# Attention and FFN on one core: the first batch's FFN units given out later, and three batches' units pinned in program order

## The chip, the cores and the metric

The kernel runs on one core of one Trainium2 chip. The metric is device time in microseconds (us) of one execution; several runs are taken and their median is quoted. The engines are named as in the profile: PE is TensorE's matmul, PEld its weight load, DVE is VectorE, ACT is ScalarE, POOL is GpSimd, and SP is SyncE, whose queue issues the DMAs.

## What is computed

Eight batches of eight heads, 576 positions, head width 64: attention weights are kept only within `tau` of the row's maximum. The result, as 4608 tokens of width 512, goes through a feed-forward network (FFN) of two layers with width 2048 between them.

```python
scores = scale * np.matmul(q, k.transpose(0, 1, 3, 2))
thresh = np.max(scores, axis=-1, keepdims=True) - tau
scores = np.where(scores >= thresh, scores, -1000000000.0)
scores = scores - np.max(scores, axis=-1, keepdims=True)
attn = np.exp(scores)
attn = attn / (np.sum(attn, axis=-1, keepdims=True) + 1e-09)
attn_out = np.matmul(attn, v)
x = np.ascontiguousarray(attn_out.transpose(0, 2, 1, 3)).reshape(B * S, H * D)
h = x @ w_in
g = h * (1.0 / (1.0 + np.exp(-h)))
out = g @ w_out
```

## The kernel before

**Attention** works in tiles of 128 query rows by 576 keys. A tile `t` goes through `scores` (PE: line 456 in batch 0, line 468 later), `soft1` (DVE, line 478: the maximum), `soft1b` (ACT, line 488: exp), `soft2` (DVE, line 497: mask, multiply and sum), `soft2b` (ACT line 515, or POOL line 511: divide by the sum) and `soft3`. In batch 0 `soft3` transposes on PE (lines 407 and 412) and copies out on ACT (lines 420 and 421); in later batches POOL splits the tile in two float16 halves (lines 523 to 529) and a DMA transposes them (line 539). `av` multiplies with V (line 430 in batch 0, line 554 later), and `av_post` (lines 572 and 573) writes a pair of heads into `x16`, the input of the FFN. `x16` has two buffers, so batch b+2 can write it only when the first layer of batch b is done. Score tiles have two PSUM buffers, exp tiles four.

**The FFN** of one range of token columns is cut in 32 units of 12 matmuls. An `h_unit` (first layer, line 597) makes one block of 128 hidden features; its `post` is tanh on ACT (line 607), a product on DVE (line 608), a float16 copy on ACT (line 614) and the rest on DVE (line 615). An `o_unit` (second layer, line 630) is a quarter of one block of 128 outputs; after the fourth quarter ACT scales it into `wst` (line 642) and SP stores it. Batches 0 and 1 come in ranges of 256 and 320 columns, the others in two of 288. From batch 1's second range on, a range's second layer is held back and handed out in turn with the next range's first layer (`held`).

**The order** is written in one loop over `t` (lines 792 to 842). There are 301 tile places: batch 0's tiles stand at 0 to 15 and 28 to 47, batch 1's at 49 to 84, then 36 a batch; 16 to 27 and 48 are empty. The loop body gives out `scores(t + 1)`, the steps of the tiles around `t`, the loads and splits that are due, and as many FFN units as `credit` allows. `credit` grows by `rate` at each place. When a range becomes ready (batch 0's at places 20 and 52, batch 1's at 69 and 89, batch 2's at 125 and 126), `rate` is set to the units listed, over the places to the next range, times 0.95; batch 0's two ranges take `RATES` instead. The weights of the two layers are loaded, decoded and split in the same loop (`W_PLAN`: the second layer's are split at places 22 to 36, lines 224 and 225).

A scheduler then orders each engine's instructions by priority and by its own clock, so an engine's order is not that of the loop: scores have a high priority, FFN units none. For batches below `PACED` the first matmul of a unit is pinned behind what stands ahead of it on PE in program order:

```python
if b < PACED and k == 0:
    tc.keep_in_program_order(mm)
```

Units of other batches may be moved ahead of scores, or behind them.

Of the kernel before, what the change touches and what calls it, by code (L numbers as in the profile page):

```python
# [24 lines left out]
NF = DFF // P  # L25
# [5 lines left out]
LOAD = 5  # L31
AV_LAG = 3
GAP, GAP1 = 12, 1
PACED = 1
RATES = (1.03, 1.45)
RATE = 0.95

W_PLAN = ((0, 0, 10, 13, 0), (16, 9, 22, 36, 0))
# [14 lines left out]
def attention_moe(  # L53
# [46 lines left out]
    for i in range(2):  # L100
        t = const.tile([P, S + 64], F32R, name=f"qstack{i}")
# [268 lines left out]
    for kind, base, n in (("low", 4096, 256), ("high", 5120, 320)):  # L370
        for i in range(2):
            t = gbuf.bitcast(F32)[:, base + 2 * n * i : base + 2 * n * (i + 1)]
# [71 lines left out]
    def scores(t):  # L444
        v, parts = tiles[t]
        s_ps = ps_s.tile([P, 2, 512], F32, tag="s", name=f"s_{t}")
        sps[t] = s_ps
        if v in direct:
            (h, i, _, _) = parts[0]
            qt, kt = direct[v]  # L450
            if visits[v][2] == "low":
                o = (h % 2) * 256 + i * P
            else:
                o = (h % 2) * 384 + (i - 2) * P
            for j in range(2):
                nc.tensor.matmul(  # L456
                    s_ps[:, j, :HALF], qt[:, o : o + P],
                    kt[:, j * HALF : (j + 1) * HALF], start=True, stop=True,
                )
            return  # L460
        seq = [
            (qstack[h % 2][:, qcol(h, i) : qcol(h, i) + P], kk)
            for h, i, _, _ in parts
            for kk in khl[h]
        ]
        for n, (lhs, kk) in enumerate(seq):
            for j in range(2):
                nc.tensor.matmul(  # L468
                    s_ps[:, j, :HALF], lhs, kk[:, j * HALF : (j + 1) * HALF],
                    start=(n == 0), stop=(n == len(seq) - 1),  # L470
                )

    def soft1(t):
        s_ps = sps[t]
        sm = sb.tile([P, 5], F32, tag="small", name=f"sm_{t}", bufs=4)
        w = sb.tile([P, S], F32, tag="w32", name=f"w32_{t}", bufs=4)
        negm = sm[:, 0:1]
        nc.vector.tensor_reduce(  # L478
            out=negm, in_=s_ps[:, :, :HALF], op=ALU.max, axis=AX.XY, negate=True
        )  # L480
        nc.vector.tensor_scalar(
            out=sm[:, 1:2], in0=negm, scalar1=-1.0, scalar2=ntau, op0=ALU.mult, op1=ALU.add
        )
        small[t] = sm
        wtile[t] = w

    def soft1b(t):
        nc.scalar.activation(  # L488
            wtile[t].rearrange("p (j c) -> p j c", j=2), sps[t][:, :, :HALF], AF.Exp,
            bias=small[t][:, 0:1],  # L490
        )

    def soft2(t):
        s_ps = sps.pop(t)
        sm, w = small[t], wtile[t]
        w3 = w.rearrange("p (j c) -> p j c", j=2)
        nc.vector.scalar_tensor_tensor(  # L497
            out=w3, in0=s_ps[:, :, :HALF], scalar=sm[:, 1:2], in1=w3,
            op0=ALU.is_ge, op1=ALU.mult, accum_out=sm[:, 2:3],
        )  # L500
        nc.vector.tensor_scalar(
            out=sm[:, 3:4], in0=sm[:, 2:3], scalar1=1e-9, scalar2=2.0**-12,
            op0=ALU.add, op1=ALU.mult,
        )
        nc.vector.reciprocal(out=sm[:, 4:5], in_=sm[:, 3:4])  # L505

    def soft2b(t):
        w = wtile[t]
        r = small.pop(t)[:, 4:5]
        if tiles[t][0] in direct and not 12 <= t < first_high + 10:  # L510
            nc.gpsimd.tensor_scalar(
                out=w, in0=w, scalar1=r, scalar2=1.0, op0=ALU.mult, op1=ALU.mult
            )
        else:
            nc.scalar.activation(w, w, AF.Copy, scale=r)  # L515
# [74 lines left out]
    def h_unit(b, c0, n, f, own=None):  # L590
# [4 lines left out]
        for c in range(NK):  # L595
            for lo_w, lo_x in ((0, 0), (0, 1), (1, 0)):
# [3 lines left out]
                )  # L600
                if b < PACED and k == 0:
                    tc.keep_in_program_order(mm)
# [20 lines left out]
    def o_unit(b, c0, n, d, quarter, own=None):  # L623
        if quarter == 0:
            po[b, c0, d] = bank([P, 512], f"o_{b}_{c0}_{d}", own)
        ps = po[b, c0, d]
        for f in range(4 * quarter, 4 * quarter + 4):
            g = gt[b, c0, f]
            for k, (lo_w, lo_g) in enumerate(((0, 0), (0, 1), (1, 0))):
                mm = nc.tensor.matmul(  # L630
                    ps[:, :n], wo(f, d, lo_w), g[:, lo_g, :n],
                    start=(f == 0 and k == 0), stop=(f == NF - 1 and k == 2),
                )
                if b < PACED and f == 4 * quarter and k == 0:
                    tc.keep_in_program_order(mm)

        def post():
            if quarter < 3:
                return

            o = wst[:, NW + d % 2, :]
            nc.scalar.activation(o[:, :n], ps[:, :n], AF.Copy, scale=moe_sc[b][:, 1:2])  # L642
            c = b * S + c0
            nc.sync.dma_start(out=outT[d * P : (d + 1) * P, c : c + n], in_=o[:, :n])

        return post
# [6 lines left out]
    def o_units(b, c0, n, owns=(None,)):  # L653
        return [
            lambda d=d, quarter=quarter: o_unit(b, c0, n, d, quarter, owns[d % len(owns)])
            for d in range(DM // P) for quarter in range(4)
        ]

    held = []

    def moe_units(b, c0, n):
        if b == 0 and c0 == 0:
            return h_units(b, c0, n, (0, 2)) + o_units(b, c0, n, (0, 2))
        if b == 0 or (b == 1 and c0 == 0 and 1 in HALVED):
            return h_units(b, c0, n) + o_units(b, c0, n)
        out = []
        if held:
            for pair in zip(h_units(b, c0, n, (0, 1)), o_units(*held.pop(), (2,))):
                out.extend(pair)
        else:  # L670
            out = h_units(b, c0, n)
        held.append((b, c0, n))
        return out
# [12 lines left out]
    start = {}  # L686
# [37 lines left out]
    NT = len(tiles)  # L724
# [17 lines left out]
    def pri(offset, f):  # L742
        def g():
            if offset == 0:
                return f()
            with tc.high_priority(offset=offset):
                return f()

        return g
# [22 lines left out]
    units = []  # L772
    post = []
    credit = 0.0
    rate = 0.0

    def run_posts():
        for f in post:
            f()
        post.clear()  # L780

    def step_unit():
        p = units.pop(0)()
        run_posts()
        post.append(p)

    def live(t):
        return 0 <= t < NT and tiles[t] is not None

    scores(0)  # L790
    t = 0
    while t < NT + 8 or units or ready or held:
        while ready and ready[0][0] <= t:
            _, b, c0, n = ready.pop(0)
            units.extend(moe_units(b, c0, n))
            nxt = [r[0] for r in ready if r[0] > t + 1]
            rate = len(units) / max(1, (nxt[0] if nxt else NT + 8) - t)
            rate *= RATE
            if b == 0:
                rate = RATES[0 if c0 == 0 else 1]  # L800
        if held and not ready and not units and t >= NT + 8:
            units.extend(o_units(*held.pop()))
        if t >= first_high + 20:
            turn[1] = 3
        if live(t):
            pri(PRI_SOFT1, lambda: soft1(t))()
        if live(t + 1):
            pri(PRI_S, lambda: scores(t + 1))()
        if live(t - 1):
            soft2b(t - 1)  # L810
        if live(t):
            pri(PRI_SOFT1, lambda: soft1b(t))()
        if live(t - 1) and tiles[t - 1][0] not in direct:
            soft3(t - 1)
        if live(t - 2) and tiles[t - 2][0] in direct:
            soft3(t - 2)
        for f in todo.pop(t, []):
            f()
        credit += rate
        if t >= NT:  # L820
            credit = max(credit, 4.0)
        if units and credit >= 1:
            step_unit()
            credit -= 1
        if live(t):
            pri(PRI_SOFT2, lambda: soft2(t))()
        for v, p, c0, n in avs.pop(t, []):
            b = visits[v][0]
            if v in direct:
                a_ps = av_direct(v, p)  # L830
            else:
                a_ps = pri(PRI_AV, lambda v=v, p=p, c0=c0, n=n: av(v, p, c0, n))()
            run_posts()
            scale = xscale if v in direct else 2.0**-12
            post.append(lambda b=b, p=p, c0=c0, n=n, a_ps=a_ps, scale=scale: av_post(b, p, c0, n, a_ps, scale))
        while units and credit >= 1:
            step_unit()
            credit -= 1
        if not units:
            credit = 0.0  # L840
            run_posts()
        t += 1
# [44 lines left out]
```

## Time and profile before

| | |
|---|---|
| median of 3 runs | 1228.99 us (1227.8 to 1229.81) |
| the profiled execution | 1226.58 us |
| its span, first to last instruction | 1224.8 us |
| PE busy | 1155.2 us, 94% of the span |
| DVE busy | 920.7 us, 75% |
| ACT busy | 808.4 us, 66% |
| POOL busy | 694.6 us, 57% |
| TensorE's granted clock, mean | 0.99 of full speed |

The profiled execution takes 1.8 us more than its span. Busy times are unions: two overlapping instructions of an engine count once. A stage's row gives its length, then each engine's busy time and, in brackets, how many instructions it ran. The k-th instruction of line 497 on DVE belongs to the k-th tile that is not empty, so its start tells when the kernel is at that tile; the stages of the rows below are cut at such starts, of tiles 28, 32, 44, 49, 52, 64, 84, 104, 125, 176 and 300.

### The profile page before, as it was taken

What the parts mean: (1) busy time and instruction counts of PE and PEld (TensorE: products, weight loads), DVE (VectorE), ACT (ScalarE), POOL (GpSimd) and SP (SyncE); (2) the same over time, 40 slices, a digit from 0 to 9 for tenths busy, and PEclk for the clock granted to TensorE, in tenths of its full rate; (3) what the DMA queues carried; (4) which work ended last, traced back from release to release, by engine and by line L of the source; (5) the groups of instructions that cost most, each with busy time, mean ns of one, the idle gap of its engine ahead of it and who ended that gap; (6) DMA issues with size and microseconds to landing.
All of it is one profiled execution on the core that took longest, in us unless ns stands there. A gap on an engine that the chain in (4) does not pass through costs nothing.

```text
span 1224.8 us, 27015 instructions
## 1 busy us (share of the span) xinstructions
PE 1155.2 (94%) x9474; PEld 902.3 (74%) x9474; DVE 920.7 (75%) x2625; ACT 808.4 (66%) x1519; POOL 694.6 (57%) x888
## 2 busy tenths in 40 slices
PE   6778998999999899999999999999999999999998
PEld 4546685777876677777877777787788877777777
DVE  7987949968989788899888888896788867333330
ACT  6679846967868676777777677785777756333331
POOL 2264226987877786877878658781787567000000
PEclk9999999999999999999999999999999999999999
DMA  9740127787896787787777748772888357100000
GB/s 313 264 133 28 51 58 180 155 167 159 152 172 128 168 148 136 146 154 172 142 145 145 162 96 171 142 136 82 137 159 141 84 103 122 26 11 16 15 11 25
DMA packets 340887, 151.73 MB, mean 124 GB/s; under 512 B 305936, under 2 KB 317200, under 8 KB 340752
## 3 DMA queue, kind: packets, MB, share of 16 engines
q1 hardware_dynamic: 340752, 150.01, 57.9%
q8 instruction: 75, 1.23, 0.4%
q14 instruction: 60, 0.49, 0.1%
HBM read 66.19 MB, written 9.44 MB: 62 GB/s over the span
## 4 chain that ended last, share of the span: by engine, by line
PE 54%; DVE 16%; DMA 9%; POOL 8%; ACT 6%; issue 6%; SPq 0%; POOLq 0%; ACTq 0%; DVEq 0%
PE o L630 20%; PE h L597 18%; PE s L468 7%; PE a L554 6%; DMA wT<-hl 5%; DVE w L497 4%; DVE sm L478 3%; DVE qstack L354 3%; POOL hl L526 2%; POOL hl L523 2%; ACT w L515 2%; ACT w L488 1%; PE s L456 1%; DMA vraw<-in_vL 1%; POOL wst L229 1%
## 5 line engine op out<-in xcount | busy, mean ns | idle before, releaser
L597 PE MATMUL h<-x,wst 128*128 128x288 f16 (+2 forms) x3072 | 423.4, 287 | 8.9 <-DVE gbuf L615 6.8
L630 PE MATMUL o<-gbuf,wst 128*128 128x288 f16 (+2 forms) x3072 | 418.5, 286 | 2.2 <-ACT wst L642 0.7
L597 PEld LDWEIGHTS <-wst 128*128 128x128 f16 x3072 | 292.1, 98 | 99.1 <-issue 21.0
L630 PEld LDWEIGHTS <-wst 128*128 128x128 f16 x3072 | 293.2, 98 | 82.3 <-issue 5.3
L526 POOL TENSOR_TENSOR hl<-w,hl 128x512 f16<-128x512 f32 x252 | 303.8, 1206 | 11.9
L523 POOL TENSOR_SCALAR hl<-w 128x576 f16<-128x576 f32 x252 | 171.7, 684 | 178.3 <-ACT w L515 140.6
L497 DVE SCALAR_TENSOR_TENSOR w<-s,sm,w 128x576 f32<-128x576 f32 x288 | 231.8, 812 | 47.1 <-ACT w L488 44.2
L488 ACT ACTIVATE w<-s,sm 128x576 f32<-128x576 f32 x288 | 210.9, 740 | 77.1 <-DVE sm L478 34.0
L478 DVE TENSOR_REDUCE sm<-s 128x1 f32<-128x576 f32 x288 | 215.2, 751 | 47.1 <-PE s L468 38.2
L515 ACT ACTIVATE w<-w,sm 128x576 f32<-128x576 f32 x266 | 201.6, 771 | 46.2 <-DVE sm L505 45.3
L607 ACT ACTIVATE th<-h,msc 128x288 f32<-128x288 f32 (+2 forms) x256 | 127.5, 499 | 110.4 <-PE h L597 109.2
L608 DVE SCALAR_TENSOR_TENSOR h<-th,h 128x288 f32<-128x288 f32 (+2 forms) x256 | 116.2, 456 | 109.9 <-ACT th L607 108.2
L468 PE MATMUL s<-khi,qstack 128*128 128x288 f32 x560 | 143.4, 336 | 9.3 <-DVE w L497 8.6
L614 ACT ACTIVATE gbuf<-h 128x288 f16<-128x288 f32 (+2 forms) x256 | 104.1, 408 | 71.9 <-DVE h L608 70.5
L615 DVE SCALAR_TENSOR_TENSOR gbuf<-h,gbuf 128x288 f16<-128x288 f32 (+2 forms) x256 | 115.3, 451 | 41.6 <-ACT gbuf L614 41.1
L554 PE MATMUL a<-wT,v 128*64 128x288 f16 (+2 forms) x1568 | 118.6, 292 | 12.9 <-DMA wT<-hl 12.7
L468 PE MATMUL s<-klo,qstack 128*128 128x288 f32 x560 | 120.7, 296 | 0.0
L364 POOL TENSOR_TENSOR klo<-kraw,khi 128x576 fp32r<-128x576 f32 x64 | 93.0, 1453 | 45.1 <-ACT khi L362 32.5
L554 PEld LDWEIGHTS <-v 128*64 128x64 f16 x1568 | 86.7, 111 | 36.8 <-issue 26.6
L468 PEld LDWEIGHTS s<-khi,qstack 128*128 128x128 f32 x560 | 87.3, 189 | 29.3 <-issue 15.3
L468 PEld LDWEIGHTS s<-klo,qstack 128*128 128x128 f32 x560 | 90.0, 188 | 0.8 <-issue 0.2
L529 POOL TENSOR_TENSOR hl<-w,hl 128x64 f16<-128x64 f32 x252 | 90.3, 358 | 0.0
(101 smaller groups left out, 905.5 us busy)
## 6 DMA issues: line engine op xcount, KB each, us to landing
kraw<-in_kT SPq DMA_DIRECT2D x128, 144.0 KB, 2.9
qraw<-in_qT SPq DMA_DIRECT2D x96, 144.0 KB, 3.0
vraw<-in_vL SPq DMA_DIRECT2D x32, 320.0 KB, 3.8
out_t<-wst SPq DMA_DIRECT2D x48, 144.0 KB, 2.1
gbuf<-in_w_in SPq DMA_DIRECT2D x12, 512.0 KB, 7.2
wT<-hl SPq DMA_TRANSPOSE x280, 3.3
wraw<-in_w_out SPq DMA_DIRECT2D x8, 512.0 KB, 4.5
gbuf<-in_w_out SPq DMA_DIRECT2D x8, 512.0 KB, 4.9
```

The lines of the kernel that those rows point to most:

```text
L468: nc.tensor.matmul(s_ps[:, j, :HALF], lhs, kk[:, j * HALF : (j + 1) * HALF], start=(n == 0), stop=(n == len(seq) - 1),)
L478: nc.vector.tensor_reduce(out=negm, in_=s_ps[:, :, :HALF], op=ALU.max, axis=AX.XY, negate=True)
L488: nc.scalar.activation(wtile[t].rearrange("p (j c) -> p j c", j=2), sps[t][:, :, :HALF], AF.Exp, bias=small[t][:, 0:1],)
L497: nc.vector.scalar_tensor_tensor(out=w3, in0=s_ps[:, :, :HALF], scalar=sm[:, 1:2], in1=w3, op0=ALU.is_ge, op1=ALU.mult, accum_out=sm[:, 2:3],)
L515: nc.scalar.activation(w, w, AF.Copy, scale=r)
L523: nc.gpsimd.tensor_scalar(out=fl[:, 0:S], in0=w, scalar1=1.0, scalar2=1.0, op0=ALU.mult, op1=ALU.mult)
L526: nc.gpsimd.tensor_tensor(out=fl[:, 640:1152], in0=w[:, 0:512], in1=fl[:, 0:512], op=ALU.subtract)
L554: nc.tensor.matmul(a_ps[odd * D : (odd + 1) * D, :n], vt[:, lo_v, odd, kv, :], wT[v, b * H + 2 * p + odd][:, kw, c0 - base : c0 - base + n ...
L597: mm = nc.tensor.matmul(ph[:, :n], wi(c, f, lo_w), x16[b, lo_x][:, c, c0 : c0 + n], start=(k == 0), stop=(k == 11),)
L607: nc.scalar.activation(th[:, :n], ph[:, :n], AF.Tanh, scale=moe_sc[b][:, 0:1])
L608: nc.vector.scalar_tensor_tensor(out=ph[:, :n], in0=th[:, :n], scalar=1.0, in1=ph[:, :n], op0=ALU.add, op1=ALU.mult,)
L630: mm = nc.tensor.matmul(ps[:, :n], wo(f, d, lo_w), g[:, lo_g, :n], start=(f == 0 and k == 0), stop=(f == NF - 1 and k == 2),)
```

## The change

Batch 0's first range is given out at 0.25 units a place in place of 1.03, its second at 1.75 in place of 1.45. The units of batches 1 and 2 take a rate of at most 1.75, which counts 16 held units too, and are pinned as batch 0's were. A held second layer is put on the list as soon as the list is empty, up to place 121 (batch 3's first tile). No instruction's work changes, and none is added or removed. The line numbers of the changed kernel are larger by one from line 35 on.

```diff
-PACED = 1
-RATES = (1.03, 1.45)
+PACED = 3
+TOP = 1.75
+RATES = (0.25, 1.75)
 RATE = 0.95
...
             nxt = [r[0] for r in ready if r[0] > t + 1]
-            rate = len(units) / max(1, (nxt[0] if nxt else NT + 8) - t)
+            more = NF if 0 < b < PACED else 0
+            rate = (len(units) + more) / max(1, (nxt[0] if nxt else NT + 8) - t)
             rate *= RATE
             if b == 0:
                 rate = RATES[0 if c0 == 0 else 1]
+            elif b < PACED:
+                rate = min(rate, TOP)
+        if held and not units and t < start[PACED, 0]:
+            units.extend(o_units(*held.pop(), (2,)))
```

The order of the engines shows what moves. In the rows, `w32_37` is tile 37's exp tile, `h_0_0_5` the sixth first-layer unit of batch 0's first range, `o_0_0_1` the second output block of that range; the last number is a buffer's.

**ACT around tile 37.** Before:

```order
L488 ACTIVATE w32_37_1508<-s_37_1459,sm_37_1507 128x576
L224 ACTIVATE wst_89<-wst_89,o_w_sc_989 128x512
L515 ACTIVATE w32_36_1456<-w32_36_1456,sm_36_1455 128x576
L614 ACTIVATE gbuf_61<-h_0_0_5_1060 128x256
L224 ACTIVATE wst_89<-wst_89,o_w_sc_989 128x512
L420 ACTIVATE wT_5_2_1429<-tm_35_1516 128x4x64
L421 ACTIVATE wT_5_2_1429<-tl_34_1469 128x128
L488 ACTIVATE w32_38_1547<-s_38_1511,sm_38_1546 128x576
L607 ACTIVATE th_0_0_6_1118<-h_0_0_6_1082,msc_0_770 128x256
L224 ACTIVATE wst_89<-wst_89,o_w_sc_989 128x512
L515 ACTIVATE w32_37_1508<-w32_37_1508,sm_37_1507 128x576
L607 ACTIVATE th_0_0_7_1150<-h_0_0_7_1105,msc_0_770 128x256
```

And in the changed kernel, from the same tile:

```order
L489 ACTIVATE w32_37_1279<-s_37_1243,sm_37_1278 128x576
L422 ACTIVATE wT_5_2_1213<-tl_33_1211 128x128
L399 ACTIVATE gbuf_61<-gbuf_61,gate_79 64x320
L608 ACTIVATE th_0_0_3_1273<-h_0_0_3_1218,msc_0_770 128x256
L225 ACTIVATE wst_89<-wst_89,o_w_sc_958 128x512
L516 ACTIVATE w32_36_1240<-w32_36_1240,sm_36_1239 128x576
L421 ACTIVATE wT_5_2_1213<-tm_35_1287 128x4x64
L489 ACTIVATE w32_38_1304<-s_38_1282,sm_38_1303 128x576
L422 ACTIVATE wT_5_2_1213<-tl_34_1253 128x128
```

Unit 3 of batch 0 stands where units 5 to 7 stood. From tile 32's exp to tile 44's, ACT had 12 instructions of line 607 and 13 of line 614; it now has 3 and 5.

**ACT around tile 47**, where batch 0's tiles end. Before:

```order
L488 ACTIVATE w32_46_1855<-s_46_1822,sm_46_1854 128x576
L421 ACTIVATE wT_6_5_1720<-tl_42_1787 128x128
L420 ACTIVATE wT_7_6_1834<-tm_43_1827 128x4x128
L614 ACTIVATE gbuf_61<-h_0_0_15_1434 128x256
L642 ACTIVATE wst_89<-o_0_0_0_1475,msc_0_770 128x256
L642 ACTIVATE wst_89<-o_0_0_1_1638,msc_0_770 128x256
L421 ACTIVATE wT_7_6_1834<-tl_43_1832 128x128
L488 ACTIVATE w32_47_1909<-s_47_1858,sm_47_1908 128x576
```

In the changed kernel, from the same tile on:

```order
L489 ACTIVATE w32_46_1543<-s_46_1522,sm_46_1542 128x576
L421 ACTIVATE wT_7_6_1534<-tm_44_1551 128x4x128
L422 ACTIVATE wT_7_6_1534<-tl_43_1532 128x128
L489 ACTIVATE w32_47_1590<-s_47_1546,sm_47_1589 128x576
L421 ACTIVATE wT_7_6_1534<-tm_45_1595 128x4x64
L422 ACTIVATE wT_7_6_1534<-tl_44_1556 128x128
L489 ACTIVATE w32_49_1653<-s_49_1627,sm_49_1652 128x576
```

The exp of tile 47 stood behind two second-layer results, each of 48 matmuls; nothing of the FFN stands ahead of it now. On PE, 348 FFN matmuls stood ahead of tile 52's scores; now 84 do.

**ACT after tile 177's exp**, in the changed kernel:

```order
L608 ACTIVATE th_2_288_12_7351<-h_2_288_12_7304,msc_2_5587 128x288
L615 ACTIVATE gbuf_61<-h_2_288_12_7304 128x288
L608 ACTIVATE th_2_288_13_7475<-h_2_288_13_7423,msc_2_5587 128x288
L615 ACTIVATE gbuf_61<-h_2_288_13_7423 128x288
L608 ACTIVATE th_2_288_14_7528<-h_2_288_14_7483,msc_2_5587 128x288
L615 ACTIVATE gbuf_61<-h_2_288_14_7483 128x288
L608 ACTIVATE th_2_288_15_7581<-h_2_288_15_7536,msc_2_5587 128x288
L615 ACTIVATE gbuf_61<-h_2_288_15_7536 128x288
L643 ACTIVATE wst_89<-o_2_0_3_7376,msc_2_5587 128x288
```

These are four of the twelve first-layer units between the exps of tiles 176 and 178, the last four of batch 2 (two units stood there before); four units of batch 3 and batch 4's first `x16` follow them, then tile 178's exp. PE has 1920 FFN matmuls ahead of tile 176's scores (2259 before) and 2249 ahead of tile 180's (2312 before). From tile 216 on the two counts differ by at most 49; ahead of tile 300's scores stand 4687 of the 6144 (4642 before).

## Rows read from the trace of the kernel before

**Rows 1.** The page's head: span, and busy time, share and instructions of PE.

```profile
span 1224.8 us, 27015 instructions
PE 1155.2 (94%) x9474; PEld 902.3 (74%) x9474; DVE 920.7 (75%) x2625; ACT 808.4 (66%) x1519; POOL 694.6 (57%) x888
```

**Rows 2.** Busy time by stage: PE, PEld, DVE, ACT, POOL; granted clock, DMA share, GB/s.

```profile
0.00:78.60 78.60, 57.78 (x345) 38.22 (x346) 66.59 (x204) 51.71 (x98) 22.48 (x34) 0.93 0.83 275
78.60:99.70 21.10, 14.51 (x93) 9.76 (x91) 12.78 (x47) 16.11 (x32) 16.84 (x18) 1.00 0.08 23
99.70:150.40 50.70, 45.87 (x295) 32.67 (x296) 43.40 (x117) 44.88 (x102) 16.02 (x15) 0.97 0.14 40
150.40:171.30 20.90, 20.90 (x182) 18.42 (x180) 8.47 (x27) 8.22 (x22) 2.99 (x4) 1.00 0.10 30
171.30:185.60 14.30, 13.45 (x107) 10.15 (x106) 10.23 (x29) 10.39 (x23) 6.50 (x9) 1.00 0.34 84
185.60:229.90 44.30, 37.46 (x271) 25.62 (x269) 41.98 (x116) 33.46 (x63) 32.60 (x39) 0.96 0.80 177
229.90:296.20 66.30, 65.02 (x553) 51.07 (x552) 52.88 (x155) 47.94 (x87) 56.26 (x72) 1.00 0.82 164
296.20:359.30 63.10, 59.56 (x527) 50.21 (x524) 59.39 (x174) 48.87 (x90) 52.53 (x66) 1.00 0.87 166
359.30:430.00 70.70, 62.93 (x511) 47.47 (x512) 59.55 (x177) 50.45 (x90) 51.14 (x66) 0.98 0.73 144
430.00:594.90 164.90, 159.84 (x1346) 125.70 (x1344) 146.57 (x424) 123.50 (x224) 126.61 (x166) 0.99 0.77 151
594.90:1035.50 440.60, 431.94 (x3725) 345.03 (x3724) 366.50 (x1049) 313.46 (x570) 306.61 (x401) 1.00 0.68 131
1035.50:1224.80 189.30, 185.93 (x1543) 148.01 (x1540) 52.33 (x118) 59.42 (x130) 3.98 (x6) 1.00 0.07 20
```

**Rows 3.** The same stages, first layer alone (line 597), then second layer alone (line 630).

```profile
99.70:150.40 50.70, 18.28 (x151) 14.82 (x152) 0.97 0.14 40
150.40:171.30 20.90, 2.29 (x20) 1.66 (x17) 1.00 0.10 30
185.60:229.90 44.30, 21.03 (x138) 13.41 (x139) 0.96 0.80 177
...
150.40:171.30 20.90, 15.02 (x132) 12.84 (x132) 1.00 0.10 30
171.30:185.60 14.30, 6.08 (x55) 5.29 (x55) 1.00 0.34 84
```

**Rows 4.** Groups by line and shape, PE, 1060 to 1200 us, and that stretch.

```profile
L630 PE MATMUL o<-gbuf,wst 128*128 128x288 f16 x581 | 76.6, 286 | 0.0
L597 PE MATMUL h<-x,wst 128*128 128x288 f16 x564 | 74.5, 286 | 0.0
...
1060.00:1200.00 140.00, 140.00 (x1145) 111.82 (x1144) 43.56 (x95) 48.49 (x106) 0.00 (x0) 1.00 0.04 14
```

**Rows 5.** Groups by line and shape, whole span: one unit's post at 256 columns.

```profile
L607 ACT ACTIVATE th<-h,msc 128x256 f32<-128x256 f32 x32 | 15.3, 480 | 3.9 <-PE h L597 3.7
L608 DVE SCALAR_TENSOR_TENSOR h<-th,h 128x256 f32<-128x256 f32 x32 | 13.4, 420 | 5.6 <-ACT th L607 5.6
L614 ACT ACTIVATE gbuf<-h 128x256 f16<-128x256 f32 x32 | 12.5, 392 | 3.2 <-DVE h L608 3.1
L615 DVE SCALAR_TENSOR_TENSOR gbuf<-h,gbuf 128x256 f16<-128x256 f32 x32 | 13.3, 414 | 0.4 <-ACT gbuf L614 0.3
```

**Rows 6.** Waits between 150.4 and 171.3 us: us in total, times, longest.

```profile
ACT wst L642 <- PE o L630: 10.0, 2, 5.2
DVE w L497 <- ACT w L488: 9.7, 4, 9.1
```

**Rows 7.** PE's own waits between 185.6 and 1035 us.

```profile
PE a L554 <- DMA wT<-hl: 12.7, 12, 2.4
PE s L468 <- DVE w L497: 8.6, 10, 2.6
```

## The prediction, made before the changed kernel ran

> **What bounds the kernel now.** I read the page's head first [rows 1]: PE is busy 1155.2 of 1224.8 us, so 69.6 us of the span are PE's idle time. No instruction is added or taken away, so the change can only move that idle time, at first order. Where it lies is read from busy time by stage [rows 2]: length less PE's busy time gives 20.8 us before 78.6 us, 6.6 up to 99.7, 4.8 up to 150.4, none up to 171.3, 0.9 up to 185.6, 6.8 up to 229.9, 1.3, 3.5 and 7.8 in the three stages up to 430, 5.1 up to 594.9, 8.7 up to 1035.5, and 3.4 in the last. The last stage is the reason why all of it counts: from 1035.5 us, with the last tiles through, PE works off the FFN for 189.3 us, 185.9 of them busy, while DVE has 52.3 us of work. A us of FFN that PE does not do earlier stands at the end, unless it fills a gap. In that part PE runs at its best: 1145 matmuls of 288 columns in 140 us without a gap [rows 4], 122 ns each, so 109 ns at 256 columns and 136 at 320.
>
> Three readings from the stages that the change touches. From 99.7 to 150.4 us (tiles 32 to 44, with the split of the second layer's weights) three engines share the load: PE 45.9, ACT 44.9 and DVE 43.4 of 50.7 us [rows 2]. From 150.4 to 171.3 us PE is never idle while DVE and ACT work 8.5 and 8.2 of 20.9 us; 132 second-layer matmuls run here [rows 3], and the waits say what stands still: ACT waits 10.0 us for second-layer results, and DVE once 9.1 us for an exp [rows 6], which is behind them in ACT's queue, as the order shows. From 185.6 to 229.9 us DVE is busy 42.0 of 44.3 us: it is the bound there, with PE idle for 6.8.
>
> **The early stretch, tiles 28 to 52.** The order shows 264 FFN matmuls fewer ahead of tile 52's scores (348 to 84), all of 256 columns: 264 x 0.109 = 28.7 us of PE's work go out and are done later. The question is whether this stretch becomes as much shorter.
> - *78.6 to 99.7 us*: ahead of tile 32's scores only 9 matmuls leave, and POOL's weight split (16.8 of 21.1 us) stays. I take 0.
> - *99.7 to 150.4 us*: by ACT's order 9 tanh and 8 copies leave, 9 x 0.480 + 8 x 0.392 = 7.5 us [rows 5]; DVE loses some 9 posts, 9 x (0.420 + 0.414) = 7.5; PE 75 matmuls, 8.2. The three fall together, so I take 7.5 us off. Least, half of it counts because the transposes, copies and scores of a tile wait for each other in turn: 4. Most, the whole stage shrinks with PE's share, 45.9 to 37.7 us at 90%: 9.
> - *150.4 to 171.3 us*: without the second-layer block what is left is DVE's work less one post, 8.5 - 0.8 = 7.6 us, the longest of the four. At 90% that takes 8.5 us, so 12.4 come off. Bounds: 10.3 (at 72%, DVE's share in the stage behind, it takes 10.6) and 13.3 (no gap).
> - *171.3 to 185.6 us*: 43 of 55 second-layer matmuls go, but DVE and ACT keep 10.2 and 10.4 us and gain a post. At 85% to 90% that is 12.2: 2.1 us off, between 0 and 3.5.
>
> Sum: 22.0 us off (14.3 to 25.8) against 28.7 us of PE's work put off. The early stretch costs 28.7 - 22.0 = **6.7 us**, between 2.9 and 14.4. Queues: SP loses two early groups of stores, which stood ahead of batch 1's loads and transposes; four stores come back around tiles 65 to 73. I count this at nothing, within the bounds.
>
> **Tiles 52 to 64.** DVE's order has the same steps of batch 1's start, and now the first range's posts in place of the second's. PE has 157 FFN matmuls in place of 156, but of 256 columns instead of mostly 320: 120 x 0.027 = 3.2 us less. The posts are shorter too, by about 0.1 us each, ten of them: 1.3 us. DVE is the bound, so **1.9 us** more of PE stay idle; between -1 and 5, the last if first-layer units wait for PSUM behind V's splits on DVE (the order puts posts 7 and 8 around them).
>
> **Tiles 64 to 176.** The pace is alike: 1679 FFN matmuls now (241 to 1920), 1755 before (504 to 2259). PE is the bound at 98%, 94%, 89% and 97% of the four stages [rows 2]; the hole is 359.3 to 430 us, 7.8 us idle, where batch 1's second range was paced at 0.475 units a place and now gets 1.478. An even supply may fill some of it. What ended PE's waits there speaks against much: 12.7 us for transposed tiles and 8.6 for a score buffer over the whole run of the attention [rows 7], neither a lack of FFN work. I take **-2 us**, between -8 and +3.
>
> **The catch-up, tiles 177 to 180.** What was put off is worked off when batch 4 needs `x16`: some 300 matmuls with few scores between. ACT's order has twelve first-layer units between two exps there. Attention stands still for 300 x 0.122 = 37 us, as it did in the block at 150.4 to 171.3 us, where PE had no gap. It costs nothing beyond work already counted, 0 to 2 us if the attention restarts slowly. From tile 216 on the counts differ by at most 49.
>
> **Sum.** 6.7 + 1.9 - 2 = **+6.6 us**. The profiled execution takes 1226.6 us, 2.4 less than the median of 1229.0; the change is added to the median: 1235.6 us. All low ends together give -6.1, all high ends +24.4.
>
> **The rivals.**
> - *Even pacing pays (faster).* Place: tiles 84 to 176, idle 16.4 us in all [rows 2]. With batches 1 and 2 pinned behind the scores, PE meets FFN units and scores alternately, and the late transposes find a unit ahead of them. It decides from about 8.6 us of recovered idle time on. If 10 come back and the early stretch costs 3 and tiles 52 to 64 nothing: -7, 1222 us. For it: idle time is clustered where the old pace was thinnest. Against: the waits named above are for data.
> - *No change.* The early stretch shrinks nearly as PE's work does (2.9), and 2 to 4 us come back later: 1229 us.
> - *Pinned units stand behind late scores (slower still).* For some 100 tiles a unit can't pass scores that wait for their buffer. If each costs what the present waits do over 12 more occasions, 12 x 0.86 = 10 us: 1246 us. Against: scores have two buffers, and batch 0's units are pinned already.
> - *The clock.* Between 0 and 78.6 us PE is busy 57.8 of 78.6 us, 74%, and the granted clock is 0.93; at 90%, from 99.7 to 150.4 us, it is 0.97 [rows 2], so part of a thin stretch is at 1.2 instead of 2.4 GHz. PE's share from tile 32 to 52 goes from 93% (80.2 of 85.9 us) to 51.5 / 63.9 = 81%. A mean of 0.93 is 14% of the time at the lower level: 9 of 63.9 us, which lose some 4.5 us of PE's work if nothing hides them: 1240 us. The Trainium skill, "TensorE: Matmul & The Clock Gate", section "HAM oscillation — how this bites in real kernels", has a rule against such a change: gaps in PE's work make the array fall back to the half rate, and the next burst starts slow. By it the early stretch would cost 11 us in place of 6.7. In this trace the 74% stretch bears it out only weakly, at a clock of 0.93.
>
> That the change doesn't do what it says is ruled out by the order: the units move as described.
>
> **How the numbers follow.** A measurement here can tell about 0.2% (2.5 us) from no change. My forecast, slower by 6.6 us, has 0.41; pinned units behind scores 0.10, the clock 0.05; no change 0.17; even pacing 0.27. Slower together 0.56, same 0.17, faster 0.27. The range reaches down to 1218, past the even-pacing case, and up to 1250, past the pinned case; less than 1 in 10 is left on either side.
>
> **What would show it.** Right: tile 52's mask (line 498 on DVE) starts near 164 us instead of 185.6; no wait of 9 us for an exp before it; PE idle time up to there near 40 us (33.1 before); a stretch near tile 178 in which PE has no gap for some 37 us and DVE works about half; tile 300's some 12 us later, as 45 matmuls fewer are left for the end. Wrong: tile 52 at 158 us or earlier, or after 170; PE idle between tiles 84 and 176 under 8 us (faster), or over 25 (pinned units); a granted clock under 0.93 between tiles 32 and 64.

## The result, and the profile after

The changed kernel takes 1246.83 us (median of 4 runs, 1242.78 to 1249.26) where the kernel before takes 1228.67 (4 runs): 1.0144 times the time, 95% interval 1.0115 to 1.0172, so 18 us slower. The profiled execution took 1242.78 us with a span of 1241.0, 16.2 us above the span of before; the ledger below is made against that.

The page's head of the changed kernel, against [rows 1]:

```profile
span 1241.0 us, 27028 instructions
PE 1157.3 (93%) x9474; PEld 904.3 (73%) x9474; DVE 921.6 (74%) x2625; ACT 810.0 (65%) x1519; POOL 688.6 (55%) x888
```

The work is the same; PE's idle time is 83.7 us in place of 69.6, and 2.1 us went into busy time. Busy time by stage of the changed kernel, columns as in [rows 2], cut at the same tiles (176 to 180 is a stage of its own here):

```profile
78.70:99.50 20.80, 14.78 (x93) 9.79 (x91) 12.23 (x47) 16.07 (x32) 16.86 (x18) 1.00 0.08 23
99.50:146.20 46.70, 36.69 (x190) 24.28 (x191) 38.51 (x100) 39.59 (x86) 14.72 (x14) 0.89 0.13 37
146.20:154.50 8.30, 7.53 (x51) 5.19 (x50) 7.12 (x25) 6.55 (x15) 3.91 (x5) 1.00 0.25 71
154.50:166.60 12.10, 9.61 (x76) 7.22 (x74) 10.38 (x30) 9.71 (x22) 7.17 (x8) 1.00 0.41 99
166.60:211.20 44.60, 33.85 (x272) 26.64 (x273) 40.94 (x117) 32.94 (x64) 34.31 (x43) 0.92 0.78 173
211.20:276.20 65.00, 61.40 (x535) 48.22 (x532) 56.55 (x157) 49.99 (x90) 56.10 (x71) 1.00 0.88 166
345.30:405.50 60.20, 58.58 (x537) 48.54 (x535) 51.45 (x152) 45.50 (x79) 53.72 (x69) 1.00 0.83 158
568.80:617.70 48.90, 48.04 (x424) 37.93 (x421) 29.09 (x71) 24.77 (x49) 9.73 (x14) 1.00 0.41 92
1057.00:1241.00 184.00, 180.68 (x1500) 143.83 (x1497) 51.08 (x115) 58.71 (x128) 4.29 (x7) 1.00 0.08 20
```

Tile 52 comes at 166.6 us in place of 185.6. The second-layer block at tile 47 is gone: 8.3 us for the stage that took 20.9. Tiles 52 to 64 take as long as before, 44.6 against 44.3 us, DVE 92% busy and PE idle for 10.7 us. The catch-up is there, 48.9 us with PE busy for 48.0. Its longest wait, in the changed kernel's trace between 568.8 and 617.7 us, shows the attention standing still:

```profile
POOL hl L524 <- DMA wT<-hl: 33.3, 1, 33.3
```

### The profile page after: what moved, and what is told of

Same layout as the page of the kernel before. It is cut to its first block, busy times and chain, and to the rows that moved or that the text cites. A ratio compares the mean times of both kernels' runs of the same rounds, so it can differ in the third digit from the quotient of the medians.

```text
span 1241.0 us, 27028 instructions
## 1 busy us (share of the span) xinstructions
PE 1157.3 (93%) x9474; PEld 904.3 (73%) x9474; DVE 921.6 (74%) x2625; ACT 810.0 (65%) x1519; POOL 688.6 (55%) x888
## 4 chain that ended last, share of the span: by engine, by line
PE 59%; DVE 17%; DMA 8%; ACT 7%; issue 5%; POOL 4%; SPq 0%; ACTq 0%; POOLq 0%; DVEq 0%
PE o L631 24%; PE h L598 19%; PE s L469 8%; PE a L555 6%; DVE w L498 4%; DVE sm L479 3%; DMA wT<-hl 3%; DVE qstack L355 3%; ACT w L516 2%; ACT w L489 2%; DMA vraw<-in_vL 1%; DVE gbuf L616 1%; DVE h L609 1%; PE s L457 1%; POOL wst L230 1%
## 5 line engine op out<-in xcount | busy, mean ns | idle before, releaser
L527 POOL TENSOR_TENSOR hl<-w,hl 128x512 f16<-128x512 f32 x252 | 299.7, 1189 | 12.2
L469 PE MATMUL s<-khi,qstack 128*128 128x288 f32 x560 | 143.4, 337 | 11.1 <-DVE w L498 10.6
L555 PE MATMUL a<-wT,v 128*64 128x288 f16 (+2 forms) x1568 | 114.5, 289 | 7.7 <-DMA wT<-hl 5.9
L555 PEld LDWEIGHTS <-v 128*64 128x64 f16 x1568 | 83.4, 109 | 31.2 <-issue 23.1
```

The lines of the kernel that those rows point to most:

```text
L469: nc.tensor.matmul(s_ps[:, j, :HALF], lhs, kk[:, j * HALF : (j + 1) * HALF], start=(n == 0), stop=(n == len(seq) - 1),)
L527: nc.gpsimd.tensor_tensor(out=fl[:, 640:1152], in0=w[:, 0:512], in1=fl[:, 0:512], op=ALU.subtract)
L555: nc.tensor.matmul(a_ps[odd * D : (odd + 1) * D, :n], vt[:, lo_v, odd, kv, :], wT[v, b * H + 2 * p + odd][:, kw, c0 - base : c0 - base + n ...
```

## Where the time went: a ledger by stretch

For each stretch I set its length beside the FFN work that PE has in it. The work is counted in PE's order (matmuls standing ahead of the scores of the first and last tile) and priced at 109, 122 or 136 ns for 256, 288 or 320 columns [rows 4]. If a stretch is bound by PE, its length falls by what is taken out; what it falls short is lost, since the work stands at the end.

| tiles | length before, after | FFN before, after | length | FFN | lost |
|---|---|---|---|---|---|
| 28 to 52 | 107.0, 87.9 | 37.8, 9.1 | -19.1 | -28.7 | 9.6 |
| 52 to 84 | 110.6, 109.6 | 60.7, 52.3 | -1.0 | -8.3 | 7.4 |
| 84 to 176 | 298.7, 292.6 | 177.8, 173.4 | -6.1 | -4.4 | -1.7 |
| 176 to 180 | 12.4, 48.9 | 6.5, 40.2 | 36.4 | 33.8 | 2.7 |
| 180 to 300 | 428.1, 439.3 | 285.0, 298.2 | 11.1 | 13.2 | -2.1 |
| 300 to the end | 189.3, 184.0 | 183.7, 178.2 | -5.3 | -5.5 | 0.2 |

Nearly all of the 16.2 us is lost ahead of tile 84: 9.6 us where the FFN was thinned, and 7.4 us behind it. What waits there is in PE's own waits of tiles 52 to 64 (us in total, times, longest), before between 185.6 and 229.9 us and in the changed kernel between 166.6 and 211.2 us, and in DVE's timeline of the first gap, with PE's line that ends it:

```profile
PE s L468 <- DVE w L497: 4.4, 3, 2.6
PE h L597 <- DVE gbuf L615: 0.8, 1, 0.8
```

```profile
PE h L598 <- DVE gbuf L616: 10.2, 4, 4.3
```

```profile
170.63 1.67 DVE L317 SCALAR_TENSOR_TENSOR v<-vraw,v_sc,v 128x640 f16<-128x640 f32 x2
172.22 0.74 DVE L479 TENSOR_REDUCE sm<-s 128x1 f32<-128x576 f32 x1
...
174.66 0.74 DVE L616 SCALAR_TENSOR_TENSOR gbuf<-h,gbuf 128x256 f16<-128x256 f32 x2
...
175.12 4.22 PE L598 MATMUL h<-x,wst 128*128 128x256 f16 x24 [4.29 <-DVE gbuf L616]
```

First-layer units wait for the last step of earlier units on DVE, which frees their PSUM bank and stands behind V's splits and the tiles' own steps. For tiles 64 to 84, where 3.9 of the 7.4 us are lost, PE is busy 94%, DVE 87% and POOL 86%; PE idles for 3.6 us, 2.3 of them in waits for transposed tiles (1.3 before). What keeps that stretch at its length isn't shown.

## The experiments

Theory L: lateness costs by PE standing idle in tiles 28 to 84. Rival P: the pins, and held layers given out alone, cost later. Four kernels take the change apart. Each ratio is against runs of the kernel before made beside it.

**Rates alone**: `RATES = (0.25, 1.75)` in the kernel before.

> Only the two rates of batch 0 (0.25 and 1.75) go in; no unit of batch 1 or 2 is pinned, no held layer is given out early, no cap. Theory L (lateness: PE stands idle in tiles 32 to 84 because its FFN work has gone from there; +13.8 us of idle by tile 84 in the changed kernel): 12 to 16 us slower than before, PE idle up to tile 84 near 55 us (41 before). Theory P (pinned units and unpaired layers cost in batches 1 and 2; lateness costs only the 6.7 us forecast): 5 to 9 us slower.

Measured: 1242.55 us, ratio 1.0140 (1.0116 to 1.0164). That is 17 us, slightly above theory L's range and far outside theory P's, and PE is idle for 54.6 us up to tile 84, as L has it. In the ledger 9.3 and 6.8 us are lost in the first two stretches. The rates alone are enough for the whole of the loss.

**Pins alone**: `PACED = 3` in the kernel before, nothing else.

> Only the pinning of batches 1 and 2 goes in; rates as before. Theory L: within 3 us of before. Theory P: 5 to 9 us slower, with waits of the first layer for its own results on VectorE (line 615) of more than 12 us in all, 6.8 before.

Measured: 1243.59 us, 1.0146 (1.0122 to 1.0170). Both theories missed: nothing is lost ahead of tile 84, and 13.5 us in tiles 84 to 176, but not by the waits named (2.5 us over the whole run). Between the scores of tiles 104 and 125 PE has 167 FFN matmuls (282 before), for batch 1's second range is paced at 0.475 a place and can no longer be moved ahead. Stage and PE's waits there:

```profile
357.00:428.00 71.00, 53.67 (x421) 40.16 (x421) 62.87 (x180) 51.68 (x93) 53.44 (x68) 0.90 0.70 146
```

```profile
PE s L468 <- DVE w L497: 8.7, 6, 4.6
PE s L468 <- DVE sm L481: 5.0, 2, 3.0
```

The stage takes 71.0 us, as before (70.7), with DVE busy for 62.9 us (59.6 before) and PE idle for 17.3 us in place of 7.8. PE waits for score buffers (0.7 us there before), and the units that could fill the time are pinned behind those scores.

**Held layer and cap alone**, rates and pins as before; against the kernel before this comes to:

```diff
+            more = NF if 0 < b < 3 else 0
...
+            elif b < 3:
+                rate = min(rate, TOP)
+        if held and not units and t < start[3, 0]:
+            units.extend(o_units(*held.pop(), (2,)))
```

> The held second layer is given out when the list is empty, with its 16 units counted in the rate and the cap of 1.75; batch 0's rates as before, no pins beyond batch 0. Theory L: within 3 us of before. Theory P (the held layer alone leaves the next first layer without a partner): 3 to 6 us slower, waits of the first layer for line 615's results above 10 us.

Measured: 1227.06 against 1225.20 us, 1.0009 (0.9988 to 1.0029): no change, as theory L has it.

**The changed kernel with pins for batch 0 alone** (`if b < 1 and ...` at both places):

> The changed kernel with pins for batch 0 alone. Theory L: 12 to 18 us slower than before, as the changed kernel. Theory P: 6 to 10 us slower, the waits between tiles 125 and 176 (6.2 us in the changed kernel) gone.

Measured: 1244.86 us, 1.0148 (1.0125 to 1.0171), 18 us, the upper end of theory L; 9.7 and 6.5 us are lost in the first two stretches. The pins cost 18 us alone and nothing here, where the pace between tiles 89 and 125 is 1.478.

The next three turn one number of the changed kernel, batch 0's rates.

**Old rates**: `RATES = (1.03, 1.45)`.

> The changed kernel (pins, held layer, cap) with batch 0's old rates 1.03 and 1.45: nothing is late. Theory L' (lateness costs by PE's early idle time; pins cost only where the pace behind them is thin, at tiles 104 to 125, which the held units now fill at 0.976 a place): within 4 us of before, PE idle between tiles 104 and 125 under 10 us (17.3 with pins alone). Rival (pins cost wherever they stand): 12 to 18 us slower than before.

Measured: 1229.88 against 1226.71 us, 1.0034 (1.0017 to 1.0051), some 4 us, the edge of theory L'; PE is idle for 7.3 us between tiles 104 and 125. So pins don't cost 18 us wherever they stand: at a pace of 0.475 a place they do, at 0.976 little is left of it, at 1.478 nothing.

**Half late**: `RATES = (0.6, 1.75)`.

> The changed kernel with 0.6 for 0.25: 214 FFN matmuls stand ahead of tile 52's scores (348 before, 84 in the changed kernel). Theory L': the cost goes with the work put off, about half: 6 to 11 us slower than before. Rival (the cost comes with the later catch-ups and restarts, whatever the amount put off): 14 to 18 us slower.

Measured: 1226.89 against 1226.71 us, 1.0021 (1.0000 to 1.0042): at most 5 us, well under half of the changed kernel's 18. Both missed: more than half of the matmuls that the changed kernel puts off are put off here, for next to nothing.

**Later still**: `RATES = (0.1, 1.75)`.

> The changed kernel with 0.1 for 0.25: 36 FFN matmuls ahead of tile 52's scores. Theory L': the early stretch hardly shrinks any more (tile 52 at 162 to 166 us, 166.6 in the changed kernel), so the further 48 matmuls, 5.2 us, are nearly all lost: 20 to 24 us slower than before. Rival: 14 to 18 us slower, as the changed kernel.

Measured: 1260.41 against 1226.71 us, 1.0285 (1.0258 to 1.0313); some 35 us slower and so outside both ranges, with tile 52 at 167.1 us. The two stretches, tiles 28 to 52 and 52 to 84, at 0.6 and then at 0.1:

```profile
76.00:169.90 93.90, 79.74 (x533) 57.66 (x531) 73.97 (x217) 77.97 (x170) 43.58 (x48) 0.98 0.17 44
169.90:277.40 107.50, 99.18 (x835) 76.50 (x835) 96.13 (x263) 79.04 (x142) 89.69 (x108) 1.00 0.85 172
```

```profile
78.40:167.10 88.70, 69.66 (x350) 44.65 (x349) 66.04 (x191) 68.76 (x142) 43.59 (x45) 0.87 0.16 43
167.10:276.20 109.10, 87.25 (x760) 72.64 (x759) 94.25 (x267) 80.13 (x144) 89.28 (x111) 0.94 0.86 170
```

| rate | FFN ahead of tile 52 | tiles 28 to 52: length, lost | FFN, tiles 52 to 84 | length, lost | time against before |
|---|---|---|---|---|---|
| 1.03 (before) | 37.8 us | 107.0 | 60.7 us | 110.6 | 1 |
| 0.6 | 23.3 | 93.9, 1.4 | 62.8 | 107.6, -5.1 | 1.0021 |
| 0.25 | 9.1 | 87.9, 9.6 | 52.3 | 109.6, 7.4 | 1.0144 |
| 0.1 | 3.9 | 88.7, 15.6 | 44.4 | 109.0, 14.8 | 1.0285 |

The table shows where the loss comes from. Each stretch has a floor of its own: near 88 us up to tile 52, near 108 up to tile 84. Above the floor, FFN work can leave and the stretch shrinks with it; at the floor each us that leaves is lost. The second stretch stands at its floor at every rate, and at 0.25 and 0.1 it also gets less FFN: the units that come there late are first-layer ones of 256 columns, each with as many DVE steps as a wider one, and fewer matmuls run there (396 at 0.1, 445 at 0.25, 462 before). What PE waits for at the floor isn't always the same: at 0.1 it waits in the second stretch for transposed tiles and score buffers, and for first-layer results only 0.3 us:

```profile
PE a L555 <- DMA wT<-hl: 8.7, 6, 2.6
PE s L469 <- DVE sm L482: 7.0, 2, 6.4
PE s L469 <- DVE w L498: 4.9, 4, 1.8
```

The 5.1 us won in the second stretch at 0.6 are mostly given back: 4.2 us are lost in tiles 84 to 176.

**What makes the second floor.** Theory D: V's splits and maxima stand in one block on DVE ahead of the first layer's results. They are pinned in program order:

```diff
-        nc.vector.scalar_tensor_tensor(
+        op = nc.vector.scalar_tensor_tensor(
             out=o[:, 1], in0=t, scalar=s, in1=o[:, 0], op0=ALU.mult, op1=ALU.subtract
         )
+        tc.keep_in_program_order(op)
```

(and the same for `vmax`; for batches 1 and 2 in the changed kernel, for all but batch 0's maximum in the other two).

> The changed kernel; V's second split and V's maximum of batches 1 and 2 are pinned in program order on VectorE, so that they no longer stand in one block ahead of the first layer's results at tiles 53 to 56. Theory D (that block holds the first layer's PSUM banks, and the gaps bring the clock down): PE idle from tile 52 to 64 falls from 10.7 us to 7 or less, time at the lower clock there from 6.8 us to 3.4 or less, and the run is 8 to 14 us slower than before, 4 to 8 better than the changed kernel. Rival (VectorE is full there in any order): within 2 us of the changed kernel.

> The kernel before with the same pins for all batches' V steps. Theory D: 2 to 5 us faster than before, PE idle from tile 52 to 64 under 5 us (6.8 before). Rival: within 2 us of before.

> 0.6 and 1.75 for batch 0, the held layer given out, FFN pins for batch 0 alone, V steps pinned in all batches. Lateness at this rate cost 2 to 3 us at most; theory D gives 2 to 5 back: from 3 us faster to 1 us slower than before. Rival: 2 to 4 us slower.

Measured: 1.0136 (1.0110 to 1.0162) on the changed kernel, 0.9993 (0.9972 to 1.0014) on the one before, 1.0021 (1.0002 to 1.0040) at 0.6. All three are the rival's; PE idles for 9.6 us in tiles 52 to 64 of the first and 8.8 of the second, where theory D had 7 and 5. Tiles 52 to 64 of the first, and what PE waits for there:

```profile
165.00:207.90 42.90, 33.35 (x269) 26.32 (x269) 40.13 (x111) 31.64 (x61) 33.65 (x42) 0.92 0.78 162
```

```profile
PE h L602 <- DVE gbuf L620: 4.9, 3, 2.4
PE s L473 <- DVE w L502: 3.7, 4, 2.0
```

The waits for the first layer's results are halved, and waits for score buffers take their place (0.4 us in the changed kernel). DVE is 94% busy here and 92% in the changed kernel. So this order of DVE's steps isn't what costs, and DVE's work is the likely floor of tiles 52 to 64; no kernel with less of that work was run, so that is a reading and not shown.

**Is the first floor PE's clock?** In the changed kernel each of tiles 32 to 47 computes one half of its scores twice:

```diff
-            for j in range(2):
+            for j in (0, 1, 0) if 32 <= t < 48 else (0, 1):
```

> The changed kernel; each of tiles 32 to 47 computes one half of its scores a second time (16 matmuls more, about 10.6 us of PE work that changes nothing). If the thin stretch is bound by ScalarE and VectorE and what hurts there is the low clock of an idle PE: time at the lower clock between tiles 32 and 52 falls from 10.2 us to 5 or less, tile 52 comes at the same time or earlier, and the run is 0 to 5 us faster than the changed kernel. If the supply of work is all that counts and the chain scores, exp, mask is what binds: tile 52 comes 5 to 10 us later and the run is 5 to 10 us slower than the changed kernel.

Measured: 1.0202 (1.0170 to 1.0233), some 7 us above the changed kernel, with tile 52 2.4 us later: neither alternative as written. Tiles 32 to 52 of this kernel, and of the changed one:

```profile
102.20:169.00 66.80, 56.76 (x338) 40.58 (x338) 55.34 (x154) 55.35 (x122) 25.46 (x26) 0.97 0.19 53
```

```profile
99.50:166.60 67.10, 53.83 (x310) 36.69 (x312) 56.01 (x154) 55.85 (x122) 25.80 (x26) 0.92 0.20 53
```

PE has 28 matmul records more here and is busy for 2.9 us more, the clock is 0.97 for 0.92, and the stretch takes the same time. This doesn't settle the question. Work and clock moved together, with opposite signs, and the time at the lower clock has gone in part to tiles 28 to 32, which take 23.8 us at 0.86 in place of 20.8 at 1.00; over tiles 28 to 52 the clock is 0.94 in both kernels.

Two earlier traces answer better. In tiles 32 to 52 PE, DVE, ACT and POOL run the same instructions in the same order in the changed kernel, with the rates alone, and in the changed kernel with pins for batch 0 alone. Only the time at the lower clock differs: 10.2 us in the first two, 13.6 us in the third. The second and the third:

```profile
98.10:164.90 66.80, 53.53 (x310) 36.74 (x310) 56.10 (x154) 55.81 (x122) 25.76 (x26) 0.92 0.19 53
```

```profile
98.80:166.00 67.20, 55.93 (x310) 37.52 (x311) 56.14 (x154) 55.68 (x122) 25.80 (x26) 0.90 0.19 52
```

3.4 us more at the lower clock add over 2 us to PE's busy time and at most 0.4 us to the stretch. So PE's clock is a small part of the first floor. DVE and ACT, at 83% each, and the steps of a tile that wait for each other are what is left; which of the two isn't separated. Why the run with the added work is slower behind tile 84 stays open; the scheduler made its order anew.

Tiles 52 to 64 have such a pair too. With the pins alone they run the order of the kernel before, with no time at the lower clock in place of 3.4 us, and take 43.6 us in place of 44.3:

```profile
184.10:227.70 43.60, 35.85 (x271) 24.82 (x269) 42.55 (x116) 33.22 (x63) 32.52 (x39) 1.00 0.81 181
```

The changed kernel is at the lower clock for 6.8 us more than the kernel before in tiles 28 to 52 and for 3.4 us more in tiles 52 to 64. Priced by these two pairs, 0.4 and 0.7 us for each 3.4, that is some 1.5 of the 17 us lost there, an estimate.

**A middle rate** (0.8 and 1.6, held layer given out, pins for batch 0 alone), tried as a version that might beat both:

> 0.8 and 1.6 for batch 0, the held layer given out, FFN pins for batch 0 alone: 272 FFN matmuls ahead of tile 52's scores (348 before, 214 at 0.6, 84 in the changed kernel). If the first part of the lateness is free, because the stretch shrinks by as much as is put off, the stretch from tile 28 to 52 takes 97 to 101 us (107.0 before) and the run is 4 us faster to 1 us slower than before. If every unit put off costs its part: 3 to 6 us slower.

Measured: 1.0032 (1.0014 to 1.0050), some 4 us slower. The time is in the second alternative's range, and the stretch to tile 52 took 101.7 us, just outside the first's: 2.9 of the 8.3 us put off are lost there. But that isn't the whole cost: tiles 52 to 84 gained 5.8 us in the ledger, as at 0.6, and 12.8 were lost in tiles 84 to 176, where PE waited 10.5 us for transposed tiles (7.0 before). No version here beats the kernel before.

## Why the prediction was right in direction and short in size

- *The bound and the argument* held: work unchanged, PE's idle time decides, and what PE does not do early stands at the end. 14.1 of the 16.2 us are PE's idle time. The time lies inside the stated range, near its upper end, and the loss is nearly three times the forecast; the range was wide enough for every rival too, so what speaks for the prediction is where the loss stands.
- *Tiles 28 to 52*: forecast 22.0 us off against 28.7 put off, 6.7 lost; measured 19.1 off, 9.6 lost, within the bounds. The block at tile 47 came out as worked (12.4 forecast, 12.6 measured). The error is in tiles 32 to 44: 7.5 us off forecast, 4.0 measured, my lower end. I priced what leaves the engines and let the stage shrink by it, where it had a floor that I did not look for.
- *Tiles 52 to 84* is **the term that failed**. It stood at 1.9 us and measured 7.4. For tiles 52 to 64 I had 1.9 us ("DVE is the bound"); the ledger has 3.4, by the wait that I had named for the upper bound, 5 us: first-layer units behind V's splits on DVE. For tiles 64 to 84 I took PE to be the bound at 98% busy and let the loss be part of the -2; it is 3.9, since the stretch keeps its length with 5.2 us of FFN less. A PE at 98% told me that PE was full, not that the stretch would shrink when PE got less.
- *Tiles 84 to 176*: -2 forecast, -1.7 measured, in part by luck: 3.6 us are lost up to tile 104, 7.2 won up to 125 and 1.8 lost behind it. *Catch-up and behind*: 0 to 2 forecast, 0.6 measured, with PE busy for 48.0 of 48.9 us.
- *The signs named*: tile 52 at 164 us (166.6), idle time up to it 40 us (39.2), tile 300 12 us later (21.5), no gap in PE at the catch-up, no long wait for an exp ahead of tile 52 (1.7 us at most, 9.1 before): right, but for the size. PE's idle time between tiles 84 and 176, 17.9 us, showed neither of the signs of being wrong there. The clock's sign of being wrong showed: 0.89 from 99.5 to 146.2 and 0.92 from 166.6 to 211.2 us, 0.92 over tiles 32 to 64. Its cost is small, some 1.5 of the 17 us lost by the estimate above.
- *The rivals*: pinned units behind late scores is what pins alone do, 18 us, but in the changed kernel the higher pace covers it. That this rival's 1246 us is the time measured is a coincidence: without those pins the changed kernel takes as long. Even pacing did win 6.2 us of PE's idle time in tiles 104 to 125 (7.8 to 1.6), with the pins or without them, and tiles 125 to 176 gave 5.2 back.

## What to carry to other kernels

When work that only fills gaps is moved, ask of each stretch how long it takes without it: that floor, not the busy share of the engine that does the work, says how much may leave for nothing. Here the first 134 matmuls cost 1.4 us in their stretch, the next 130 another 8. A pin on an instruction cost nothing here while the pace behind it was high, and 18 us where the list ran thin, since it took away the scheduler's right to fill a gap.

## What was not expected of the hardware

The spread of one kernel's runs mostly goes with TensorE's granted clock. In 80 executions of the kernel before, the mean clock lay between 0.982 and 0.996; the 14 at 0.992 or more have a median of 1223.6 us, the 12 at 0.986 or less 1228.6. That holds within three of the four series of executions; in the fourth, of 17 with a clock of 0.985 to 0.993, no such relation shows, and which of the two causes the other isn't shown. A single profile compares kernels to no better than some 5 us, and the verdicts above are those of the medians; the ledger rests on single profiles, but kernels that run the same order in a stretch agree there within 1 us.
